# Attention and a mixture of experts on one core: the subtractions that form the low parts of the second-layer weights, moved from GpSimd to VectorE for experts 2 to 7

## The chip, the cores and the metric

The kernel runs on one core of one Trainium2 chip. The metric is the device time of one execution in microseconds; for the kernel before, three runs were timed. A separate execution was taken with the hardware profiler, and every time of the trace is counted from the start of its span.

## The reference, cut to what matters

Eight batches of 2496 tokens with 256 channels go through an attention whose weights are squared positive scores. Each of the 19968 resulting rows that passes a skip test is given to one of eight experts, a two-layer network of 256, 1024 and 256 channels, and the expert's output is added with a gate.

```
scores = (1 / S) * z @ z.T ; attn = maximum(scores, 0) ** 2
x = u * (attn @ v)
xc = x[x @ w_skip > 0]
e_idx = argmax(xc @ w_gate) ; gate_w = softmax(xc @ w_gate)[e_idx]
for e in range(8):
    h = maximum(xc[e_idx == e] @ w1[e], 0)
    y[e_idx == e] = gate_w * (h @ w2[e])
out[x @ w_skip > 0] = xc + y
```

All is float32. The kernel gets near that accuracy by splitting each matmul operand into a high part (a cast to the fp32r format) and a low part (the rest) and by adding three products: high by high, high by low, low by high.

## The kernel before, in words

**Two stages.** The attention goes through 40 chunks of up to 512 queries (to about 1250 us of the trace). Routing writes the tokens' numbers and gates into one list per expert in DRAM. Then the experts are worked through one after the other.

**An expert.** Of each expert's list, the first 768 tokens are worked in three *fixed units* of 256 tokens (NFIX = 3, `unit(e, 4, ...)`, i = 0, 1, 2), and the rest in the arm of a `tc.Switch` (line 1034) on the number of further blocks of 64 tokens, in units of up to 512 tokens. All five engines branch at the Switch; each loads the arm's number (line 1027) and gives a prefetch hint (line 1028) in the third fixed unit.

**A unit.** `fetch` (lines 639 and 641) copies token numbers to `go` on VectorE, and GpSimd gathers the rows xgf or xgu by indirect DMA. `turn_pe` (lines 659 to 662) transposes them on TensorE into pst; ScalarE writes the high part xt and VectorE the low part. Then `h_part` p computes psh with 24 matmuls for a fixed unit (line 693; four psh buffers), ScalarE writes hh (line 698) and VectorE hl (line 699). `y_part` adds up the second layer in y (line 712). VectorE forms o (line 741) and GpSimd scatters it into the output by indirect DMA (line 744). For a fixed unit the order is h0, h1, h2, h3, y0, y1, y2 and y3 in one; these are the slots 0 to 6, and a table `fills` hangs other work behind a slot.

**Weights.** While expert e is worked, the weights of e + 1 are brought in eight pieces by `load_w` (called once per expert; the pieces are hung behind slots 1, 3 and 5 of the fixed units). Pieces 0 to 3 are w1, pieces 4 to 7 are w2. For a piece, SP loads a raw tile of 128 x 512 (line 97, four raw buffers, three pieces ahead); ScalarE casts the high part (line 152 for w1h, 158 for w2t); the low part is a subtraction (line 153 for w1l, one of 128 x 512; line 159 for w2t, two of 128 x 256). The engine of the subtraction is `load_w`'s second argument:

```
wq = load_w(e + 1, nc.gpsimd if e else nc.vector) if more else []
```

So the weights of experts 0 and 1 have their subtractions on VectorE, those of experts 2 to 7 on GpSimd. For e from 1 to 6 the pieces 0 to 2 stand in the first fixed unit, 3 to 5 in the second (piece 4 behind slot 3, piece 5 behind slot 5), 6 and 7 in the third (behind slots 1 and 3).

**The order of the work.** The schedule is manual: each engine runs its instructions in the order in which the code writes them, so an instruction that waits holds up all that its engine has behind it.

## Time and profile before

| what | value |
|---|---|
| three timed runs | 1748.35, 1749.15, 1760.32 us; median 1749.15 |
| the profiled execution | 1752.5 us, span 1750.7 us, mean clock 0.997 |
| attention stage (0 to 1218 us) | TensorE busy 1208.1 us, VectorE 982.6, ScalarE 941.3, GpSimd 257.1 |
| one expert (1354 to 1412 us) | TensorE busy 58.0 of 58 us, VectorE 21.4, ScalarE 19.1, GpSimd 35.2 |
| another (1474 to 1543 us) | TensorE busy 67.8 of 69 us, VectorE 27.7, ScalarE 21.9, GpSimd 37.8 |

In the tables of the profile, PE is TensorE, PEld its weight loads, DVE VectorE, ACT ScalarE, POOL GpSimd and SP the engine that issues most DMAs. A row of a timeline gives the start, the duration, the engine, the line, the operation, the tiles written and read, how many are merged in the row, and in brackets the idle time of that engine just before and what ended it. "issue" means that nothing that the profile shows ended it.

### The profile page before, as it was taken

The numbers are of one execution on the slowest core, as the hardware profiler recorded it, in microseconds if no ns is written. First come the engines' busy times: TensorE is split into PE (matmuls) and PEld (weight loads), VectorE is DVE, ScalarE is ACT, GpSimd is POOL, SyncE is SP. The second block draws the span as 40 slices with busy tenths as digits, with TensorE's granted clock in tenths as the row PEclk, the third lists the DMA queues.
The fourth block names the chain that finished last, engine by engine and source line by source line (L and its number), as shares of the span: only waits on it lengthen the run. The fifth ranks groups of instructions, "written<-read, shape, count | busy, mean of one in ns | idle before, by whom it ended". The sixth has DMA issues, their size and how long they took to land.

```text
span 1750.7 us, 39411 instructions
## 1 busy us (share of the span) xinstructions
PE 1725.2 (99%) x15474; PEld 1526.5 (87%) x15474; DVE 1204.1 (69%) x1976; ACT 1111.2 (63%) x1409; POOL 516.6 (30%) x516
## 2 busy tenths in 40 slices
PE   9999999999999999999999999999999999999998
PEld 7888889988888898888988887888889989999997
DVE  7877877887787788788878877877743334343432
ACT  8877876887687688778768875877333323333321
POOL 1103202211220321132132112112346546645731
PEclk9999999999999999999999999999999999999999
DMA  5586699589869957986896899589543324323210
GB/s 188 151 219 176 174 255 282 145 227 256 210 155 251 278 156 220 266 222 154 247 257 167 217 273 230 144 223 241 163 117 86 90 79 106 91 60 95 85 41 27
DMA packets 424972, 307.32 MB, mean 176 GB/s; under 512 B 187888, under 2 KB 362865, under 8 KB 424016
## 3 DMA queue, kind: packets, MB, share of 16 engines
q1 hardware_dynamic: 410592, 280.44, 59.0%
q0 software_dynamic: 13632, 22.99, 4.7%
q8 instruction: 137, 2.24, 0.5%
q14 instruction: 179, 1.47, 0.3%
q10 hardware_dynamic: 432, 0.18, 0.0%
HBM read 184.21 MB, written 140.08 MB: 185 GB/s over the span
## 4 chain that ended last, share of the span: by engine, by line
PE 86%; DMA 7%; ACT 2%; issue 2%; DVE 2%; SPq 0%; another core or an unknown queue 0%; POOL 0%; POOLq 0%; DVEq 0%; ACTq 0%
PE acc L421 53%; PE y L712 11%; PE psh L693 11%; PE ps L302 8%; DMA r<-kept 3%; DMA out<-o,idt 2%; DMA out<-xr 1%; PE psm L493 1%; PE pst L659 1%; DVE al L392 1%; ACT ah L388 1%; PE ps L285 0%; ACT r L379 0%; DMA raw<-in_v 0%; ACT r L378 0%
## 5 line engine op out<-in xcount | busy, mean ns | idle before, releaser
L421 PE MATMUL acc<-ah,vh 64*128 64x512 f32 (+1 forms) x3120 | 640.4, 384 | 3.7 <-DVE ah L388 2.5
L421 PE MATMUL acc<-ah,vl 64*128 64x512 f32 (+1 forms) x3120 | 625.6, 382 | 0.0
L392 DVE TENSOR_TENSOR al<-r,ah 128x1024 fp32r<-128x1024 f32 (+1 forms) x400 | 479.7, 1205 | 152.6 <-ACT ah L388 128.3
L421 PE MATMUL acc<-al,vh 64*128 64x512 f32 (+1 forms) x3120 | 497.8, 384 | 3.4 <-DVE al L392 3.1
L592 POOL DMA_INDIRECT lst<-pair,dest x160 | 199.5, 1247 | 781.0 <-DVE dest L590 752.2
L388 ACT CAST ah<-r 128x1024 fp32r<-128x1024 f32 (+1 forms) x356 | 362.9, 1029 | 105.6 <-DMA r<-kept 71.9
L421 PEld LDWEIGHTS acc<-ah,vh 64*128 64x128 f32 x3120 | 325.7, 184 | 55.2 <-DVE ah L388 3.7
L421 PEld LDWEIGHTS acc<-ah,vl 64*128 64x128 f32 x3120 | 326.1, 184 | 44.1 <-DVE vl L122 0.3
L421 PEld LDWEIGHTS acc<-al,vh 64*128 64x128 f32 x3120 | 308.1, 184 | 58.8 <-DVE al L392 13.8
L378 ACT ACTIVATE r<-ps 128x1024 f32<-128x1024 f32 (+1 forms) x224 | 228.0, 1018 | 127.8 <-PE ps L302 112.1
L698 ACT ACTIVATE hh<-psh 128x512 fp32r<-128x512 f32 (+2 forms) x172 | 96.1, 572 | 290.9 <-PE psh L693 243.9
L379 ACT ACTIVATE r<-r 128x1024 f32<-128x1024 f32 (+1 forms) x224 | 235.9, 1053 | 7.1
L712 PE MATMUL y<-w2t,hh 128*128 128x256 f32 (+1 forms) x1328 | 237.6, 282 | 0.6 <-issue 0.4
L699 DVE SCALAR_TENSOR_TENSOR hl<-psh,hh 128x512 fp32r<-128x512 f32 (+2 forms) x172 | 110.0, 655 | 155.7 <-ACT hh L698 112.7
L712 PEld LDWEIGHTS y<-w2t,hh 128*128 128x128 f32 (+1 forms) x1328 | 202.6, 187 | 3.0 <-issue 0.9
L319 DVE STREAM_TRANSPOSE rt<-r 128x512 f32<-128x512 f32 x304 | 197.4, 687 | 11.1 <-DMA kept<-rt 11.1
L693 PE MATMUL psh<-xt,w1h 128*128 128x256 f32 (+3 forms) x896 | 185.1, 304 | 7.1 <-DVE hl L699 4.5
L712 PE MATMUL y<-w2t,hl 128*128 128x256 f32 (+1 forms) x664 | 185.4, 279 | 0.7 <-DVE hl L699 0.7
L693 PEld LDWEIGHTS psh<-xt,w1h 128*128 128x128 f32 x896 | 141.9, 189 | 13.2 <-DVE hl L699 5.9
L693 PE MATMUL psh<-xt,w1l 128*128 128x256 f32 (+3 forms) x448 | 135.3, 302 | 0.0
L744 POOL DMA_INDIRECT out<-o,idt x77 | 76.5, 994 | 167.3 <-DVE o L741 134.4
L712 PEld LDWEIGHTS y<-w2t,hl 128*128 128x128 f32 (+1 forms) x664 | 123.8, 186 | 0.9 <-DVE hl L699 0.9
(197 smaller groups left out, 1740.2 us busy)
## 6 DMA issues: line engine op xcount, KB each, us to landing
kept<-rt SPq DMA_DIRECT2D x304, 256.0 KB
r<-kept SPq DMA_DIRECT2D x90, 512.0 KB
r<-kept SPq DMA_DIRECT2D x62, 352.0 KB
raw<-in_v SPq DMA_DIRECT2D x80, 256.0 KB
ut<-in_uT SPq DMA_DIRECT2D x32, 512.0 KB
xr<-xrow SPq DMA_DIRECT2D x128, 128.0 KB
out<-xr SPq DMA_DIRECT2D x32, 512.0 KB
raw<-in_w SPq DMA_DIRECT2D x64, 256.0 KB
```

The lines of the kernel that those rows point to most:

```text
L302: nc.tensor.matmul(to, k[h, o : o + P], queries(ci, q, h, n), start=(m == 0), stop=(m == 2))
L319: nc.vector.transpose(t[:, :, 32 * k : 32 * k + 32].rearrange("p (k a) i -> p a k i", k=4), r[:, x, :].rearrange("p (a k i) -> p a k i", a ...
L378: nc.scalar.activation(r[:, :, :n], ps[:, :, :n], AF.Relu, scale=isc)
L379: nc.scalar.activation(r[:, :, :n], r[:, :, :n], AF.Square)
L388: (nc.scalar.copy if on_act(ci, p) else nc.vector.tensor_copy)(h_, r_)
L392: nc.vector.tensor_sub(l_, r_, f32(h_))
L421: nc.tensor.matmul(acc[t][:, :n], w[h, x, dd], a[h, x, :n], start=(first and t not in halves[:m]), stop=(last and t not in halves[m + 1 :]),)
L592: put = nc.gpsimd.indirect_dma_start(out=lst, out_offset=bass.IndirectOffsetOnAxis(ap=dest[:, t : t + 1], axis=0), in_=pair[:, t, :], in_o ...
L693: nc.tensor.matmul(ps[:, j * W : (j + 1) * W], wt[:, a, o : o + P], x[:, d, :W], start=(m == 0), stop=(m == 5),)
L698: nc.scalar.activation(hh[:, : G * W], ps[:, : G * W], AF.Relu)
L699: nc.vector.scalar_tensor_tensor(hl[:, : G * W], ps[:, : G * W], 0.0, f32(hh[:, : G * W]), op0=ALU.max, op1=ALU.subtract)
L712: nc.tensor.matmul(ys[t], h[:, tt], w2t[f][:, k, :], start=(f == 0 and m == 0 and t % share == 0), stop=(f == NF - 1 and m == 2), skip_gro ...
```

## The change

The second-layer subtraction is no longer given to the engine that `load_w` is called with; it always goes to VectorE. The w1 pieces keep their engine: GpSimd for experts 2 to 7.

```
                     nc.scalar.copy(t[:, 0, :], r[:, a, :])
-                    eng.tensor_sub(t[:, 1, :], r[:, a, :], f32(t[:, 0, :]))
+                    nc.vector.tensor_sub(t[:, 1, :], r[:, a, :], f32(t[:, 0, :]))
```

For six experts with four w2 pieces of two subtractions each, that is 48 instructions. TensorE, ScalarE and SP keep their order.

On VectorE, from the second half of expert 1's second fixed unit into its third (idt_203 and idt_202 are the token lists of experts 2 and 1; xt_17906 is a tile of turned rows):

```order
 L699 SCALAR_TENSOR_TENSOR hl<-psh,hh 128x512 x2
 L662 TENSOR_TENSOR xt_17906<-pst,xt_17906 128x2x256
+L159 TENSOR_TENSOR w2t<-raw,w2t 128x256 x2
 L639 COPY go<-idt_203 128x2
+L159 TENSOR_TENSOR w2t<-raw,w2t 128x256 x2
 L741 SCALAR_TENSOR_TENSOR o<-y,idt_202,xgf 128x256 x2
 L1027 TENSOR_LOAD arm
 L699 SCALAR_TENSOR_TENSOR hl<-psh,hh 128x512 x2
 L639 COPY go<-idt_202 128x2
+L159 TENSOR_TENSOR w2t<-raw,w2t 128x256 x2
 L1028 SWITCH_STRIDE
 L1028 ISA
```

Pieces 4 and 5 stand ahead of an index copy and of o; piece 6 stands between the second hl and the third, which follows the hint.

Later in the same third unit on VectorE (from its third hl to the second turned tile for the Switch):

```order
 L699 SCALAR_TENSOR_TENSOR hl<-psh,hh 128x512 x2
 L662 TENSOR_TENSOR xt_17907<-pst,xt_17907 128x2x256
+L159 TENSOR_TENSOR w2t<-raw,w2t 128x256 x2
 L639 COPY go<-idt_203 128x2
 L662 TENSOR_TENSOR xt_17907<-pst,xt_17907 128x2x256
```

Piece 7 stands between the two turned tiles.

On GpSimd, the same stretch (xgf and xgu are gathered rows, out the scatter):

```order
 L153 TENSOR_TENSOR w1l<-raw,w1h 128x512
-L159 TENSOR_TENSOR w2t<-raw,w2t 128x256 x2
 L641 DMA xgf<-xr,go 128x256 x2
-L159 TENSOR_TENSOR w2t<-raw,w2t 128x256 x2
 L744 DMA out<-o,idt_202 19968x256 x2
 L1027 TENSOR_LOAD arm
 L641 DMA xgu<-xr,go 128x256 x2
-L159 TENSOR_TENSOR w2t<-raw,w2t 128x256 x2
 L1028 SWITCH_STRIDE
 L1028 ISA
 L1028 BRANCH_PREFETCH_HINT
-L159 TENSOR_TENSOR w2t<-raw,w2t 128x256 x2
```

All four pairs are gone; of the tensor work, w1l stays between the gathers and scatters.

## The prediction

> **What bounds the kernel now.** I read the page's busy times first, then the busy times by stage from the stage where the changed instructions run, then who waited for whom there, then the ends of the idle spells one by one.

> ```profile
> PE 1725.2 (99%) x15474; PEld 1526.5 (87%) x15474; DVE 1204.1 (69%) x1976; ACT 1111.2 (63%) x1409; POOL 516.6 (30%) x516
> ```

> TensorE works nearly always; GpSimd's 30% is a mean over two unlike stages. The stage that matters runs from about 1300 us (first Switch) to 1693 us (end of the last expert's fixed units): all 48 affected subtractions lie in it, as their row below shows (1346.6 to 1648.9 us). The columns are length, then busy us (and count) of PE, PEld, DVE, ACT and POOL, then clock and DMA.

> ```profile
> 1300.00:1693.00 393.00, 386.66 (x3130) 379.56 (x3129) 151.15 (x286) 125.16 (x252) 211.32 (x218) 1.00 0.30 83
> 1693.00:1751.00 58.00, 51.07 (x394) 48.66 (x392) 18.59 (x32) 11.47 (x20) 13.73 (x14) 0.98 0.11 34
> 1412.00:1474.00 62.00, 60.17 (x457) 57.56 (x456) 22.56 (x41) 19.05 (x38) 35.65 (x38) 0.97 0.34 91
> ```

> In the stage TensorE is idle for 393.00 - 386.66 = 6.3 us only. VectorE is busy 151.15/393 = 38%, GpSimd 54%. No engine but TensorE is near a bound. The tail after 1693 us belongs to the last expert, which loads no weights for a successor, so the change has no instruction there. What ended TensorE's 6.3 us (the waits of that stage, PE rows; total, times, longest):

> ```profile
> PE psh L693 <- DVE hl L699: 4.5, 3, 1.8
> PE psh L693 <- issue: 1.8, 1, 1.8
> ```

> 4.5 + 1.8 = 6.3: four waits hold all of it. None is for GpSimd, for a gather or for a weight tile. One of them lies behind expert 0's Switch:

> ```profile
> 1302.33 0.67 PE L693 MATMUL psh<-xt,w1h 128*128 128x448 f32 x2 [1.50 <-DVE hl L699]
> ```

> Expert 0's code forms expert 1's weights on VectorE already, so this 1.50 us is no business of the change; 6.3 - 1.5 = 4.8 us in three waits are left. These follow late starts of ScalarE behind a Switch; the rows of two of them, and of a Switch without such a wait:

> ```profile
> 1417.70 2.06 ACT L698 ACTIVATE hh<-psh 128x512 fp32r<-128x512 f32 x4 [3.73 <-issue]
> ...
> 1478.38 1.85 ACT L698 ACTIVATE hh<-psh 128x448 fp32r<-128x448 f32 x4 [4.11 <-issue]
> ...
> 1357.46 1.59 ACT L698 ACTIVATE hh<-psh 128x512 fp32r<-128x512 f32 x3 [2.65 <-issue]
> ```

> The idle time in brackets is ScalarE's, and "issue" says that nothing in the profile released it. Where it is 3.73 and 4.11 us, all four psh buffers are full and TensorE waits; where it is 2.65 us (a Switch of the same kind, one expert earlier), TensorE does not. So what is left to gain here is ScalarE's branch time, not GpSimd's work.

> **The change part by part.**

> ```profile
> L159 POOL TENSOR_TENSOR w2t<-raw,w2t 128x256 fp32r<-128x256 f32 x48 | 34.2, 742 | 0.3
> L153 POOL TENSOR_TENSOR w1l<-raw,w1h 128x512 fp32r<-128x512 f32 x24 | 30.9, 1302 | 0.5
> ...
> L159 DVE TENSOR_TENSOR w2t<-raw,w2t x16: 415/419/423, 1218.4 to 1294.9; 128x256 fp32r<-128x256 f32 x16
> ```

> Removed from GpSimd: 48 subtractions of 742 ns, 34.2 us busy; its share of the stage falls from 54% to (211.3 - 34.2)/393 = 45%. Added to VectorE: 48 of the same shape; the 16 that it already runs took 419 ns, so 48 x 0.419 = 20.1 us, and its share rises from 38% to 44%. The DMAs, ScalarE's casts and TensorE's order stay as they are. GpSimd keeps the 24 subtractions w1l of 1.30 us.

> What this costs on the path is decided by what stands behind the subtractions in VectorE's queue. Per expert there are four pairs. Two (pieces 4 and 5) stand where VectorE next has a tiny index copy and then the end of a unit. The tight ones are pieces 6 and 7, in the third fixed unit: piece 6 stands ahead of the third hl, piece 7 ahead of the second xt. Here is that place in one expert (VectorE, ScalarE's casts, then the chain with TensorE's groups):

> ```profile
> 1403.80 0.16 DVE L639 COPY go<-idt 128x2 int32<-128x2 int32 x1
> 1404.60 0.69 DVE L699 SCALAR_TENSOR_TENSOR hl<-psh,hh 128x512 fp32r<-128x512 f32 x1 [0.65 <-ACT hh L698]
> 1406.30 0.69 DVE L699 SCALAR_TENSOR_TENSOR hl<-psh,hh 128x512 fp32r<-128x512 f32 x1 [1.00 <-issue]
> 1407.03 0.69 DVE L662 TENSOR_TENSOR xt<-pst,xt 128x512 fp32r<-128x512 f32 x1
> 1407.64 0.16 DVE L639 COPY go<-idt 128x2 int32<-128x2 int32 x1
> 1409.62 0.69 DVE L662 TENSOR_TENSOR xt<-pst,xt 128x512 fp32r<-128x512 f32 x1 [1.82 <-ACT xt L661]
> ```

> ```profile
> 1403.05 0.70 ACT L158 CAST w2t<-raw 128x256 fp32r<-128x256 f32 x2
> ```

> ```profile
> 1405.78 2.74 PE y L712 x24
> 1408.52 0.44 PE pst L659 x4
> 1408.96 2.74 PE y L712 x24
> 1411.70 0.44 PE pst L659 x4
> 1412.14 0.93 PE psh L693 x4
> ```

> Piece 6: its casts end at 1403.75, the index copy at 1403.96. A pair of subtractions takes at most 2 x 0.42 = 0.84 us, so it ends at 1404.80 and the third hl starts at 1404.80 instead of 1404.60: 0.2 us late. That hl is read by the y group that starts at 1408.96; it would end at 1405.5, over 3 us ahead. The fourth hl starts at 1406.30 as before. Piece 7: it follows the xt at 1407.03, ends at about 1408.6, and the second xt starts at 1409.62 as before, ending 1.8 us before the Switch's first psh at 1412.14. Cost on the path: 0.0 us. The work that hides it is TensorE's own y groups; were they gone, the cost would be 6 experts x 2 pairs x 0.84 = 10 us.

> What the relief of GpSimd is worth: it works far behind its place in the code.

> ```profile
> 1400.69 1.31 POOL L153 TENSOR_TENSOR w1l<-raw,w1h 128x512 fp32r<-128x512 f32 x1
> 1401.94 1.44 POOL L159 TENSOR_TENSOR w2t<-raw,w2t 128x256 fp32r<-128x256 f32 x2
> ```

> The pair at 1401.94 is piece 4, which belongs to the second fixed unit and runs in the third. Its gathers and scatters will now go out up to 8 x 0.71 = 5.7 us sooner per expert. But no wait of TensorE in the stage ends with a gather, so this is worth 0.0 us too. The raw buffers of w2 come free sooner as well; the last of w1's subtractions stays on GpSimd, and it is that one which frees the buffer of piece 7.

> [...] The rows: a VectorE subtraction with two SBUF inputs takes 684 ns in the median and up to 1101; one of the long ones ran under a GpSimd cast. The index copy, 0.16 us above, took 1.28 us under a w1l. Two subtractions of the very kind that is moved, under a gather, took 0.75 together, no more than alone.

> ```profile
> L122 DVE TENSOR_TENSOR vl<-raw,vh x80: 647/684/1101, 5.1 to 1092.2; 128x512 fp32r<-128x512 f32 x80
> ```

> ```profile
> 288.05 1.10 DVE L122 TENSOR_TENSOR vl<-raw,vh 128x512 fp32r<-128x512 f32 x1
> ```

> ```profile
> 287.52 1.09 POOL L263 CAST zqh<-zh 128x512 fp32r<-128x512 f32 x1 [8.29 <-PE ps L285]
> ```

> ```profile
> 1453.66 1.28 DVE L639 COPY go<-idt 128x2 int32<-128x2 int32 x1
> ```

> ```profile
> 1453.59 1.30 POOL L153 TENSOR_TENSOR w1l<-raw,w1h 128x512 fp32r<-128x512 f32 x1
> ```

> ```profile
> 1294.57 0.75 DVE L159 TENSOR_TENSOR w2t<-raw,w2t 128x256 fp32r<-128x256 f32 x2
> ```

> ```profile
> 1294.46 1.00 POOL L641 DMA_INDIRECT xgf<-xr,go  x1 [0.30 <-issue]
> ```

> So a moved pair can be held by a w1l that runs: bounds 0 and 1.30 us. I take near 0 for most: GpSimd has 24 w1l against 24 pairs, and busy with them only 30.9 of 393 us. Even the full 1.30 at piece 6 makes the third hl 1.5 us late, inside its 3 us. [...]

> Sum against the profiled execution: 1752.5 us (span 1750.7 and 1.8 around it) + 0.0 + 0.0 = 1752.5. It lies 3.35 us above the median of the three runs, 1749.15, so for a median I forecast **1749 us**, own range 1745 to 1753 for shifts of the three waits by a microsecond each.

> **The rivals.**
> *Faster by the Switch.* GpSimd's gathers leave the DMA queues sooner, and ScalarE's code for the arm arrives sooner. Then the three waits vanish: -4.8 us, and the dip of the clock behind the longest one (0.97 over 62 us, 1.9 us): 1749.1 - 6.7 = 1742.4 us. For it: 3.73 and 4.11 us against 2.65 show that ScalarE's time behind a Switch varies. Against: ScalarE's row names no releaser, and GpSimd works on through the quiet Switch too. [...]

> *Slower by the Switch.* VectorE's longer and GpSimd's shorter code shift what is fetched when, and the three quiet Switches of experts 1, 4 and 6 stall like the worst: 3 x (1.8 + 1.9) = 11.1 us, 1760 us. It decides from a gap of ScalarE somewhere between 2.65 and 3.73 us on. Against: ScalarE's instructions do not change.

> [...]

> *The change does not do what it says*: the pairs wait on VectorE for ScalarE's casts or the raw DMA, and the index copies and gathers behind them come late. Then GpSimd gains nothing, but TensorE still never waited for a gather: 1749 us again.

> **How the numbers follow.** Hidden altogether 0.75 (1749 us), hidden though the pairs wait 0.04 (the same time), faster by the Switch 0.09 (1742.4), slower by the Switch 0.07 (1760), by the port 0.05 (1762). The range 1742 to 1757 holds the first three and reaches towards the slower ones; it leaves out most of the last two. A measurement of this kernel tells about 1% (17.5 us) from no change. None of the cases gets there; 0.02 for faster and 0.03 for slower are left for what no row shows, 0.95 for the same.

> **What would show it.** In the changed kernel L159 on GpSimd is gone and on VectorE counts 64 with a median near 0.42 us; a few pairs stretch towards 1.7 us under a w1l. TensorE's idle time from 1300 to 1693 us stays near 6 us and sits behind Switches. GpSimd's w1l and gathers start sooner. I am wrong if TensorE waits for hl or xt inside a fixed unit, if a w2t pair is named as what TensorE waits for, or if the waits behind the Switches grow or go.

## The result and the profile after

| kernel | median | runs | lowest to highest |
|---|---|---|---|
| before | 1750.88 us | 20 | 1746.73 to 1760.32 |
| changed | 1766.35 us | 20 | 1757.6 to 1772.59 |

The ratio is 1.0086, with a 95% interval of 1.0076 to 1.0096: 15.5 us slower. That is inside the 1% that the forecast called "the same" and outside its range of times (1742 to 1757). The profiled execution took 1764.64 us with a span of 1762.8 us, against 1752.5 and 1750.7 before, so 12.1 us of span are there to be explained.

The page of the changed kernel, and the instructions of the moved line (count; shortest, median and longest in ns; first and last start):

```profile
PE 1730.4 (98%) x15474; PEld 1534.1 (87%) x15474; DVE 1219.3 (69%) x2024; ACT 1111.6 (63%) x1409; POOL 485.5 (28%) x468
```

```profile
L159 DVE TENSOR_TENSOR w2t<-raw,w2t x64: 411/418/1732, 1214.7 to 1657.9; 128x256 fp32r<-128x256 f32 x64
```

The move itself is as forecast: 48 instructions have left GpSimd (516 to 468; 516.6 to 485.5 us busy) and joined VectorE (1976 to 2024), with a median of 418 ns. TensorE has the same 15474 matmuls. Now the stage of the experts to the end of the last fixed units, and the tail, in the columns of the prediction's table:

```profile
1300.00:1705.00 405.00, 391.55 (x3123) 382.69 (x3124) 165.18 (x332) 124.77 (x252) 177.70 (x168) 0.99 0.28 77
1705.00:1763.00 58.00, 51.23 (x395) 48.83 (x393) 18.80 (x32) 11.63 (x21) 13.14 (x14) 0.96 0.11 34
```

TensorE is idle for 405.00 - 391.55 = 13.5 us of the stage, where it was 6.3. What ended these waits (PE rows; total, times, longest):

```profile
PE y L712 <- issue: 6.7, 10, 1.0
PE psh L693 <- DVE hl L699: 3.4, 3, 2.4
PE psh L693 <- issue: 3.3, 3, 1.9
PE pst L659 <- issue: 0.8, 1, 0.8
```

The two psh rows, the waits behind Switches, add up to 6.7 us, as good as the 6.3 of before. New are 6.7 + 0.8 us in eleven short waits inside the y groups and the turn next to them, and nothing in the profile released them. They lie in third fixed units. Nine of the eleven (6.4 of the 7.5 us) stand before matmuls whose records name no semaphore to wait for, and neither do those of the weight loads that go with them: there TensorE waited for no tile at all, it stood still. One such place, in expert 4, on ScalarE, TensorE and GpSimd:

```profile
1527.59 0.60 ACT L698 ACTIVATE hh<-psh 128x512 fp32r<-128x512 f32 x1 [1.65 <-PE psh L693]
1528.08 0.71 ACT L158 CAST w2t<-raw 128x256 fp32r<-128x256 f32 x2
1533.46 1.09 ACT L698 ACTIVATE hh<-psh 128x512 fp32r<-128x512 f32 x2 [4.68 <-remote]
```

```profile
1527.85 0.28 PE L693 MATMUL psh<-xt,w1l 128*128 128x256 f32 x1
...
1531.98 0.28 PE L712 MATMUL y<-w2t,hl 128*128 128x256 f32 x1 [0.75 <-issue]
1532.10 0.28 PE L712 MATMUL y<-w2t,hh 128*128 128x256 f32 x1
1533.43 0.47 PE L712 MATMUL y<-w2t,hh 128*128 128x256 f32 x1 [1.05 <-issue]
```

```profile
1524.74 1.01 POOL L641 DMA_INDIRECT xgf<-xr,go  x1 [0.16 <-DVE o L741]
1526.06 1.01 POOL L641 DMA_INDIRECT xgf<-xr,go  x1 [0.30 <-issue]
1527.37 1.03 POOL L744 DMA_INDIRECT out<-o,idt  x1 [0.31 <-issue]
1528.71 1.00 POOL L744 DMA_INDIRECT out<-o,idt  x1 [0.31 <-issue]
1530.02 1.05 POOL L641 DMA_INDIRECT xgu<-xr,go  x1 [0.30 <-issue]
1531.38 1.01 POOL L641 DMA_INDIRECT xgu<-xr,go  x1 [0.30 <-issue]
```

The third hh waits for the psh whose last matmul started at 1527.85 (a psh of a fixed unit takes 12 matmuls in the trace, not the 24 of the text ahead of the prediction), and starts at 1533.46: 5.6 us later, with ScalarE idle for 4.68 of them. VectorE's hl follows. TensorE's two waits here, of 0.75 and 1.05 us, do not: they stand before matmuls that name no semaphore. And TensorE's signals themselves are late. Of the four that follow the one at 1527.57 on record, the first came at 1533.44 and the last at 1533.65, though the matmuls that send them had ended from 1528.13 to 1529.98. So the late hh and TensorE's idle time stand side by side, as two signs of something that held TensorE. The granted clock was 0.83 over the 10 us from 1530. GpSimd meanwhile issues six gathers and scatters in an unbroken run, one every 1.3 to 1.4 us; in the kernel before a pair of subtractions stood in this run:

```profile
1522.48 1.01 POOL L641 DMA_INDIRECT xgf<-xr,go  x1 [0.31 <-issue]
1523.52 1.43 POOL L159 TENSOR_TENSOR w2t<-raw,w2t 128x256 fp32r<-128x256 f32 x2
1525.11 1.04 POOL L744 DMA_INDIRECT out<-o,idt  x1 [0.17 <-issue]
```

The sum, from 1270 to 1730 us, in the changed kernel and in the one before:

```profile
1270.00:1730.00 460.00, 442.92 (x3499) 431.25 (x3498) 190.98 (x388) 142.09 (x287) 201.81 (x191) 0.99 0.29 81
```

```profile
1270.00:1730.00 460.00, 452.37 (x3615) 442.12 (x3614) 180.27 (x345) 144.81 (x291) 236.02 (x241) 0.99 0.30 82
```

TensorE's idle time went from 7.6 to 17.1 us. Behind the longer spells the granted clock is lower for some microseconds; six of the 46 stretches of 10 us are under 1.00 in the changed kernel, the first and the last of them being

```profile
1280.00:1290.00 10.00, 7.24 (x50) 6.66 (x49) 2.96 (x7) 3.33 (x9) 5.28 (x5) 0.89 0.55 143
...
1530.00:1540.00 10.00, 8.21 (x57) 8.00 (x57) 3.33 (x7) 2.76 (x6) 4.06 (x4) 0.83 0.56 161
```

(1 - clock) x 10 us adds up to 6.8 us over these six, against 3.5 in the kernel before. 9.5 us more idle and 3.3 us more at the lower clock are 12.8 us, against the 12.1 of the spans. So the loss is idle spells of TensorE and the clock behind them, most of it in third units. But 2.3 of the 9.5 us lie between 1270 and 1300 us, in expert 0, where both kernels run the same instructions; they are not the change's.

### The profile page after: what moved, and what is told of

It is laid out like the page before. It is cut to its first block, busy times and chain, and to the rows that moved or that the text cites. A ratio compares the mean times of both kernels' runs of the same rounds, so it can differ in the third digit from the quotient of the medians.

```text
span 1762.8 us, 39410 instructions
## 1 busy us (share of the span) xinstructions
PE 1730.4 (98%) x15474; PEld 1534.1 (87%) x15474; DVE 1219.3 (69%) x2024; ACT 1111.6 (63%) x1409; POOL 485.5 (28%) x468
## 4 chain that ended last, share of the span: by engine, by line
PE 86%; DMA 5%; issue 4%; ACT 2%; DVE 2%; SPq 1%; POOL 1%; another core or an unknown queue 0%; POOLq 0%; ACTq 0%; DVEq 0%
PE acc L421 53%; PE y L712 11%; PE psh L693 10%; PE ps L302 8%; DMA out<-o,idt 2%; DMA r<-kept 2%; PE psm L493 1%; PE pst L659 1%; DMA raw<-in_v 1%; DVE al L392 1%; ACT ah L388 1%; PE ps L285 0%; DMA out<-xr 0%; ACT r L379 0%; ACT r L378 0%
## 5 line engine op out<-in xcount | busy, mean ns | idle before, releaser
L698 ACT ACTIVATE hh<-psh 128x512 fp32r<-128x512 f32 (+2 forms) x172 | 96.2, 572 | 311.0 <-PE psh L693 238.7
L712 PE MATMUL y<-w2t,hh 128*128 128x256 f32 (+1 forms) x1328 | 239.4, 282 | 5.9 <-issue 5.9
L699 DVE SCALAR_TENSOR_TENSOR hl<-psh,hh 128x512 fp32r<-128x512 f32 (+2 forms) x172 | 110.2, 655 | 175.6 <-ACT hh L698 130.1
L712 PEld LDWEIGHTS y<-w2t,hh 128*128 128x128 f32 (+1 forms) x1328 | 203.5, 187 | 9.5 <-issue 7.2
L319 DVE STREAM_TRANSPOSE rt<-r 128x512 f32<-128x512 f32 x304 | 197.3, 687 | 10.8 <-DMA kept<-rt 10.8
L693 PE MATMUL psh<-xt,w1h 128*128 128x256 f32 (+3 forms) x896 | 186.5, 305 | 6.7 <-DVE hl L699 3.4
L712 PE MATMUL y<-w2t,hl 128*128 128x256 f32 (+1 forms) x664 | 185.8, 280 | 3.8 <-issue 3.0
L693 PEld LDWEIGHTS psh<-xt,w1h 128*128 128x128 f32 x896 | 143.0, 190 | 13.8 <-issue 5.2
L693 PE MATMUL psh<-xt,w1l 128*128 128x256 f32 (+3 forms) x448 | 136.0, 304 | 0.0
L712 PEld LDWEIGHTS y<-w2t,hl 128*128 128x128 f32 (+1 forms) x664 | 123.9, 187 | 3.9 <-issue 2.9
```

Source lines behind the costliest of these rows:

```text
L319: nc.vector.transpose(t[:, :, 32 * k : 32 * k + 32].rearrange("p (k a) i -> p a k i", k=4), r[:, x, :].rearrange("p (a k i) -> p a k i", a ...
L693: nc.tensor.matmul(ps[:, j * W : (j + 1) * W], wt[:, a, o : o + P], x[:, d, :W], start=(m == 0), stop=(m == 5),)
L698: nc.scalar.activation(hh[:, : G * W], ps[:, : G * W], AF.Relu)
L699: nc.vector.scalar_tensor_tensor(hl[:, : G * W], ps[:, : G * W], 0.0, f32(hh[:, : G * W]), op0=ALU.max, op1=ALU.subtract)
L712: nc.tensor.matmul(ys[t], h[:, tt], w2t[f][:, k, :], start=(f == 0 and m == 0 and t % share == 0), stop=(f == NF - 1 and m == 2), skip_gro ...
```

## The experiments

Every experiment was timed beside the kernel before on the same chip; the kernels of one set shared a chip. Ratios are to the kernel before of the set, with 95% intervals.

### One half of the move at a time

Theory A: GpSimd, relieved, reaches its gathers and scatters sooner, and these meet the prefetch hints of the third fixed unit. Theory B: VectorE's 20 us more hold up hl and xt. Theory C: the subtractions on VectorE contend with GpSimd's tensor work. `pool_pad` keeps GpSimd's load beside the changed kernel; nobody reads what it writes:

```
                     nc.vector.tensor_sub(t[:, 1, :], r[:, a, :], f32(t[:, 0, :]))
+                    if eng is nc.gpsimd:
+                        nc.gpsimd.tensor_sub(scr[0][:, 0, :D], r[:, a, :], f32(t[:, 0, :]))
```

> The changed kernel, with GpSimd still running 48 subtractions of the same inputs at the old places, into a scratch tile that nobody reads; VectorE forms the real low parts. So VectorE has the whole new load and GpSimd none of the relief. Theory A (the time is lost because GpSimd, relieved, issues its gathers and scatters sooner and in one burst, into the stretch of the third fixed unit in which the engines give their prefetch hints): about 1751 us, as before. Theory B (the added 20 us on VectorE hold up hl and xt): about 1766 us. [...]

Measured: 1740.62 us against 1742.85, ratio 0.9981 (0.9965 to 0.9998). VectorE's load costs nothing where GpSimd is as busy as before. B and C fall, as far as this set goes; A's 1751 us, as the kernel before, is what came.

`act_low` relieves GpSimd and gives VectorE nothing; it leaves the low parts of the second-layer weights of experts 2 to 7 out:

```
+                    if eng is nc.gpsimd:
+                        nc.scalar.mul(t[:, 1, :], r[:, a, :], 0.0)
+                    else:
                         nc.vector.tensor_sub(...)
```

> The changed kernel, but for experts 2 to 7 the low part of w2 is neither subtracted on GpSimd nor on VectorE: ScalarE writes it as the raw tile times zero, so the low parts of these second layers are left out of the result. GpSimd is relieved, VectorE gets nothing. Theory A: slow like the changed kernel, about 1766 us (ScalarE's 48 x 0.41 = 20 us stand behind its own casts). Theory B and theory C: about 1751 us, unless ScalarE's own load delays hh, which would show as waits for hh inside the fixed units.

Measured: 1744.09 us, 1.001 (0.999 to 1.0031). The relief alone cost nothing here either, though the run of six gathers and scatters was as unbroken as in the changed kernel. So theory A, which had 1766 us here, fell too, and I took that to mean that only both together cost something. That set had no run of the changed kernel itself, which the next one made good.

### Without the hints

Both kernels without the prefetch hint of line 1028. The page of the kernel before has two DMA queues of the kind "instruction":

```profile
q8 instruction: 137, 2.24, 0.5%
q14 instruction: 179, 1.47, 0.3%
```

In expert 2 the engines run their hints from 1400.7 to 1406.1 us. In the 10 us from 1400.7 on six packets of these queues move, in the 10 us ahead of it none. What a branch waits for, no row shows. The edit:

```
-                add(fills, (1, lambda: tc.switch_hint({g: n for g in ENGINES}, narms, label="rest%d" % e)))
...
-        for arm in tc.Switch(n, narms, hint="rest%d" % e):
+        for arm in tc.Switch(n, narms):
```

> [...] Theory A with the hints as the thing that is collided with: the gaps inside the third fixed unit vanish (5 to 7 us of PE idle), but every Switch costs more: so nearer to the kernel before without hints than the 15 us between the two kernels with hints. If the difference between this kernel and the kernel before without hints is still about 15 us, the hints have no part in it.

> The kernel before without the prefetch hints: the control for the changed kernel without them. All theories: slower than 1751 us by what a branch without a hint costs in eight experts (an estimate of 0 to 3 us each from ScalarE's 2.65 to 4.11 us behind a Switch, so 1751 to 1775 us). Theory A: within 5 us of the changed kernel without hints. Theories B and C: 15 us faster than it.

Measured: changed without hints 1777.66 us, 1.0209 (1.016 to 1.0257); before without hints 1766.21 us, 1.0131 (1.009 to 1.0171). TensorE's largest wait from 1270 to 1730 us, first of the changed, then of the kernel before:

```profile
PE psh L693 <- issue: 29.4, 7, 6.5
```

```profile
PE psh L693 <- issue: 22.5, 8, 4.2
```

The hint is worth about 23 us to the kernel before. Without it the change costs 11.5 us, 6.9 of them (29.4 - 22.5) in these waits at the Switches. That is another place than the y groups, where neither of these two profiles has a wait; whether the loss there needs the hint, this set doesn't tell.

### The changed kernel on a second chip, code, operands and place of the hint

> The changed kernel once more, with nothing edited, on the chip of the three that follow. The loss needs both GpSimd without the pairs' work and the subtractions on VectorE: VectorE's load alone gave 0.9981 and GpSimd's relief alone 1.001. Three theories are left for why. F, code: VectorE's program is 56 instructions longer and GpSimd's 56 shorter, so what is fetched as code, and when, changes. G, place of the hints: the code that the hint calls in the third fixed unit arrives while GpSimd issues six gathers and scatters without a break, and TensorE is silent for 4 to 7 us there. H, VectorE's reading: a subtraction that reads two operands of SBUF on VectorE while GpSimd prepares indirect DMAs holds GpSimd or TensorE up. All three expect 1.0086 here, within 1.005 to 1.012, and in the profile PE idle spells of about 0.5 to 1 us in pairs in the y groups of third units. If it comes out within 1.003 of before, the loss hangs on the chip.

Measured: 1748.26 us against 1743.42, 1.0027 (1.0011 to 1.0044), on chip 10; the chip of the first result isn't on record. (The 56 instructions of this expectation and of one below are 48 in the trace.) The ratio is within the 1.003 named for the case that the loss hangs on the chip, and it took the ground from under the first set: `pool_pad` and `act_low` had been compared with a loss that perhaps wasn't there. Its profile has none of the paired spells in y groups: of 10.8 us of idle time between 1270 and 1730 us, 9.2 stand behind Switches, where TensorE waits for hl. The same place as above, on ScalarE, TensorE and GpSimd:

```profile
1517.45 0.60 ACT L698 ACTIVATE hh<-psh 128x512 fp32r<-128x512 f32 x1 [0.81 <-PE psh L693]
1517.94 0.70 ACT L158 CAST w2t<-raw 128x256 fp32r<-128x256 f32 x2
1518.86 0.60 ACT L698 ACTIVATE hh<-psh 128x512 fp32r<-128x512 f32 x1 [0.22 <-PE psh L693]
1520.27 0.60 ACT L698 ACTIVATE hh<-psh 128x512 fp32r<-128x512 f32 x1 [0.81 <-PE psh L693]
```

```profile
1518.54 0.28 PE L693 MATMUL psh<-xt,w1l 128*128 128x256 f32 x1
```

```profile
1515.04 1.01 POOL L641 DMA_INDIRECT xgf<-xr,go  x1 [0.16 <-issue]
...
1521.71 1.02 POOL L641 DMA_INDIRECT xgu<-xr,go  x1 [0.30 <-issue]
```

The program is the same, GpSimd's run (six from 1515.04 to 1521.71) is the same, and the third hh starts 0.32 us behind its matmul in place of 5.6. So the late hh isn't made by the program alone. The small loss of this set, as far as one profile tells, lies behind Switches, at another place than the first one.

`dve_one` (experts 2 to 7 get raw times zero, one operand, in the place of the subtraction; their second layer's low parts are left out), `pool_stub` (the changed kernel with GpSimd subtracting 2 columns at the old places) and `hint3` (the hint behind slot 3):

```
+                    if eng is nc.gpsimd:
+                        nc.vector.tensor_scalar_mul(t[:, 1, :], r[:, a, :], 0.0)
```

```
+                    if eng is nc.gpsimd:
+                        nc.gpsimd.tensor_sub(scr[0][:, 0, :2], r[:, a, :2], f32(t[:, 0, :2]))
```

```
-                add(fills, (1, lambda: tc.switch_hint(
+                add(fills, (3, lambda: tc.switch_hint(
```

> The changed kernel, but for experts 2 to 7 VectorE writes the low part of a second-layer weight as its raw value times zero: an instruction with one operand from SBUF in the place of the subtraction's two, at the same place in the program, with the same waits for the cast but for the one on the copy. The low parts of these experts' second-layer weights are left out. H expects the loss gone: 0.998 to 1.003. F, with the same number of instructions on every engine, expects it kept: 1.006 to 1.012. G expects it kept where the durations are alike (the row of the new operation will tell; if it takes half of the 0.42 us, VectorE's hint comes 0.2 to 0.4 us sooner, and G allows 1.000 to 1.009).

> The changed kernel with GpSimd subtracting 2 columns of the same operands in place of 256, at the old places of the subtractions, into scratch that nobody reads: GpSimd keeps its 56 instructions and their waits for ScalarE's casts, but is relieved of nearly all their time. F expects the loss gone, since GpSimd's program is as long as before: 0.998 to 1.002, as with the full-size dummy subtractions (0.9981). H expects it kept, since GpSimd spends its time on indirect DMAs as in the changed kernel: 1.005 to 1.010. G expects what the distances between the gathers become: if the six still go in one unbroken run of 1.3 us each, 1.005 to 1.010, and if the waits for the casts break the run as before, 0.998 to 1.003.

> The changed kernel with the hint two y groups later: at slot 3 of the third fixed unit in place of slot 1, so that the code is fetched some 6 us later, behind most of GpSimd's run of gathers and scatters and still some 10 us ahead of the Switch. G expects the loss gone or mostly so: 0.997 to 1.004, and no silence of TensorE's semaphore over 4 us around the hint's fetch. F and H expect 1.005 to 1.012, with the silent spells where they were. A new loss at the Switches (a fetch that is late there) would show as PE gaps of over 1 us at the Switch's lines and is told apart by that.

Measured: 1.002 (1.0 to 1.0039), 1.0007 (0.9993 to 1.0021) and 1.0029 (1.0012 to 1.0046). `pool_stub` lies under the control, though the intervals overlap; the other two can't be told from a control of 1.0027. The ranges on record for F, G and H were made for a loss of 0.86%. That F's holds `pool_stub`, H's `dve_one`, and G's, with its conditions, all three numbers, says nothing here: the set was too quiet to rule on the spells of the first profile.

### Which pairs, and code or waits

> The changed kernel once more, unedited, as the control of the three that follow. It gave 1.0086 when it was first timed and 1.0027 on another chip. In the two profiles the loss has two forms: idle time of TensorE (between 1270 and 1730 us 17.1 us in the first, 10.8 in the second, 7.6 in the kernel before) and, behind the longer spells, stretches at a granted clock of 0.78 to 0.99 (worth 6.8, 5.1 and 3.5 us). If the size hangs on the chip, 1.002 to 1.009 here; if the first figure was the odd one, 1.001 to 1.004.

Measured: 1746.28 us against 1742.01, 1.0017 (1.0004 to 1.0031).

`late67` and `early45` (k < 6 in the place of k >= 6) move one half of the pairs each; `pool_free` is `pool_stub` with a write of 2 columns that waits for nobody:

```
-                    eng.tensor_sub(t[:, 1, :], r[:, a, :], f32(t[:, 0, :]))
+                    (nc.vector if k >= 6 else eng).tensor_sub(t[:, 1, :], r[:, a, :], f32(t[:, 0, :]))
```

```
-                        nc.gpsimd.tensor_sub(scr[0][:, 0, :2], r[:, a, :2], f32(t[:, 0, :2]))
+                        nc.gpsimd.memset(scr[0][:, 0, :2], 0.0)
```

> Of the changed kernel only the pairs of pieces 6 and 7 stay on VectorE, the two that lie around the hint in the third fixed unit of experts 2 to 7; those of pieces 4 and 5, in the second unit, go back to GpSimd. Place theory: the loss comes from the third unit, where GpSimd's gathers and scatters run without a break around the hint and GpSimd comes to the Switch early, so all of the control's loss is here: within 0.0015 of its ratio. Sum theory: what counts is GpSimd's or VectorE's total, so about half of the control's loss: 1.001 to 1.002 if the control is at 1.0027, 1.003 to 1.005 if it is at 1.0086.

> The other half: pieces 4 and 5 on VectorE, pieces 6 and 7 back on GpSimd, so that the third fixed unit of experts 2 to 7 is as in the kernel before. Place theory: no loss, 0.998 to 1.001. Sum theory: about half of the control's loss.

> The changed kernel with GpSimd writing 2 columns of zeros to scratch at each of the old places: as many instructions as with the 2-column subtractions (1.0007), but with no operand from ScalarE's cast, so without the waits. Code theory (GpSimd's shorter program is what costs): as the 2-column subtractions, 0.999 to 1.002. Waits theory (a GpSimd that no longer waits for ScalarE's casts runs ahead to its gathers, and that costs): as the control, 1.002 to 1.009.

Measured: `late67` 1.0036 (1.0022 to 1.005), `early45` 0.9989 (0.9975 to 1.0003), `pool_free` 1.0022 (1.0008 to 1.0035). `early45` is where the place theory had it; `late67` lies above the range of both theories (the place theory allowed 0.0015 from the control's 1.0017). In this set the small loss is with the pairs of pieces 6 and 7, and GpSimd's instructions without their waits don't take it away; the intervals of `late67`, `pool_free` and the control overlap. That spoke for a GpSimd that runs ahead, and for the way that remained, the Switch.

### GpSimd held back at the Switch

In the profiles up to here, ScalarE's time behind the Switch of expert 2 was long where GpSimd's branch came right behind its own, and short where GpSimd came late: TensorE idled there for 0.8 to 2.2 us in seven runs with GpSimd's branch 4.5 to 4.9 us behind TensorE's, and for 0.0 to 0.5 us in four with 6.8 us or more. So GpSimd was delayed there by copies within scratch, ten (`after_l10`, and `before_l10` on the kernel before) or six (`after_l6`):

```
                 add(fills, (7, lambda: turn_pe(pair(e + 1, 0), turned(e + 1, 0))))
+                if e:
+                    add(fills, (7, lambda: [nc.gpsimd.tensor_copy(scr[0][:, 1, :], scr[0][:, 0, :]) for _ in range(10)]))
```

> The changed kernel, unedited, as the control of the three that follow. Between 1.0017 and 1.0027 as on the last two chips, or 1.0086 as on the first, if this chip is like it.

> The changed kernel with ten copies of 128x512 within scratch on GpSimd (0.8 to 0.9 us each by the rows of the cast of that size) at the end of the third fixed unit of experts 1 to 6, ahead of its last scatter. Switch theory: what costs on these chips is that a GpSimd without the pairs comes to the Switch 4.5 us behind TensorE's branch, right behind ScalarE's at 2.1 and VectorE's at 2.9, so that the code of three engines is fetched at once and ScalarE resumes 4 to 6 us behind its branch in place of 2.5 to 3; hh is late then, TensorE idles up to 3 us in the unit behind the Switch, and its clock falls behind the longer spells. At expert 2 the profiles so far show an idle spell of 0.0 to 0.5 us in four runs in which GpSimd's branch came 6.8 us or more behind TensorE's, and of 0.8 to 2.2 in seven in which it came at 4.5 to 4.9. It expects GpSimd's branch at 9 us or later here, ScalarE's resumption within 2.5 to 3.9 us at experts 1 to 4, and 0.997 to 1.000, under the control by 0.002 or more. Third-unit theory: what costs is that the gathers and scatters ahead of the Switch run without a break, which this edit leaves as it is: the control's ratio, and if the late scatter holds up o, more.

> The same with six copies: GpSimd's branch at about 7 to 8 us behind TensorE's. Switch theory: between the control and the kernel with ten copies, nearer to the latter (0.998 to 1.001). Third-unit theory: the control's ratio.

> The kernel before with the same ten copies. There GpSimd's branch comes at 4.6 to 5.6 us behind TensorE's too, and TensorE idled 1.5, 0, 1.8, 1.2, 0, 1.8 and 0 us behind the Switches of experts 0 to 6. Switch theory: 0.997 to 1.000 here as well, since it isn't the change that brings the loss but the place of GpSimd's branch. Third-unit theory: 1.000 to 1.003, for the late scatter alone.

Measured: control 1.0008 (0.999 to 1.0025), `after_l10` 1.001 (0.9996 to 1.0025), `after_l6` 1.0004 (0.9989 to 1.0019), `before_l10` 0.9997 (0.9983 to 1.001). The control has hardly a loss to take away, so that `after_l6` and `before_l10` lie in the Switch theory's ranges means little, but the mechanism can be read all the same. ScalarE and GpSimd of `after_l10` at expert 2:

```profile
1409.93 2.07 ACT L698 ACTIVATE hh<-psh 128x512 fp32r<-128x512 f32 x4 [5.12 <-PE psh L693]
```

```profile
1404.87 6.71 POOL L1029 COPY scr<-scr 128x512 f32<-128x512 f32 x10
1412.27 1.05 POOL L744 DMA_INDIRECT out<-o,idt  x1 [0.69 <-DVE hl L699]
```

and ScalarE of the control:

```profile
1408.60 2.07 ACT L698 ACTIVATE hh<-psh 128x512 fp32r<-128x512 f32 x4 [5.40 <-PE psh L693]
```

GpSimd is held back until 1412, and ScalarE is as late as in the control (5.12 and 5.40 us idle, four hh at once). The Switch theory falls; what it rested on was an agreement of eleven profiles at one place.

### The large loss again

> The changed kernel, unedited, on one more chip. Chip theory: the size of the loss belongs to the chip. In the profile of the first timing (1.0086) ScalarE starts hh 1.7 to 3.8 us behind the last matmul that it waits for at seven places of the expert stage, and in the profiles of three other chips (1.0027, 1.0017, 1.0008) at one place, none and none. It expects 1.000 to 1.003 here with none or one such place, or, on a chip like the first, 1.006 to 1.011 with five or more of them. If the ratio comes out above 1.005 without such places, or under 1.003 with five of them, the theory falls.

> The pairs of pieces 4 and 5 alone on VectorE, once more, beside the changed kernel and with more rounds; it gave 0.9989 [0.9975, 1.0003]. Place theory (the loss comes with the pairs of pieces 6 and 7 in the third fixed unit): 0.998 to 1.000 on any chip, also on one like the first, where the late starts of hh lie in third units. If it is slower than 1.001, the place theory falls; if it is under 0.999 with its whole interval under 1, it is a version that beats both kernels.

Measured: the changed kernel 1767.18 us against 1750.95, 1.0086 (1.0069 to 1.0104), the first result over again; `early45` 1762.77 us, 1.0076 (1.0055 to 1.0096), against 0.9989 in the third set. Call a start late where ScalarE takes up a tile of TensorE over 1.5 us behind both the last matmul that signals and its own work before. Between 1270 and 1730 us the control has seven, `early45_b` six; in the profile of the first result there were seven, in the kernel before none, in the other three controls one, none and none. Waits before matmuls that name no semaphore, in y groups and turns from 1300 us on, stand at 12 places in the control, at 11 in `early45_b`, at nine in the first result's profile, and at none in the other 17 profiles. So the size goes with both signs, and both belong to the set. That leaving the third unit alone would avoid them, the place theory, falls. The same place in the two runs of `early45`, ScalarE and GpSimd; in the last set

```profile
1524.50 0.60 ACT L698 ACTIVATE hh<-psh 128x512 fp32r<-128x512 f32 x1 [1.65 <-PE psh L693]
1524.99 0.70 ACT L158 CAST w2t<-raw 128x256 fp32r<-128x256 f32 x2
1530.37 1.09 ACT L698 ACTIVATE hh<-psh 128x512 fp32r<-128x512 f32 x2 [4.68 <-remote]
```

```profile
1525.63 1.00 POOL L744 DMA_INDIRECT out<-o,idt  x1 [0.31 <-issue]
1526.93 1.04 POOL L641 DMA_INDIRECT xgu<-xr,go  x1 [0.30 <-issue]
1528.28 1.01 POOL L641 DMA_INDIRECT xgu<-xr,go  x1 [0.30 <-issue]
1529.31 1.42 POOL L159 TENSOR_TENSOR w2t<-raw,w2t 128x256 fp32r<-128x256 f32 x2
```

and in the third set:

```profile
1507.95 0.60 ACT L698 ACTIVATE hh<-psh 128x512 fp32r<-128x512 f32 x1 [0.81 <-PE psh L693]
1508.45 0.70 ACT L158 CAST w2t<-raw 128x256 fp32r<-128x256 f32 x2
1509.36 0.60 ACT L698 ACTIVATE hh<-psh 128x512 fp32r<-128x512 f32 x1 [0.22 <-PE psh L693]
```

In `early45` VectorE has none of the moved pairs in the third unit, and still hh is late there. What differs from the kernel before at this place is GpSimd alone: without the pairs of pieces 4 and 5 its six gathers and scatters follow one another without a break.

The sets that had the changed kernel:

| set | before | changed | ratio | late starts | TensorE signals on record, of 1365 | of these late |
|---|---|---|---|---|---|---|
| first result | 1750.88 | 1766.35 | 1.0086 | 7 | 1274 | 37 |
| second chip | 1743.42 | 1748.26 | 1.0027 | 1 | 1366 | 0 |
| third | 1742.01 | 1746.28 | 1.0017 | 0 | 1367 | 0 |
| fourth | 1739.08 | 1741.33 | 1.0008 | 0 | 1365 | 0 |
| last | 1750.95 | 1767.18 | 1.0086 | 7 | 1294 | 43 |

The sixth column counts the trace's semaphore records for the signals that TensorE's instructions carry (the end of the program adds up to two). The profile of the kernel before that the prediction rests on has 1278, and `early45_b` 1284: the four profiles of the first and the last set lack 5 to 7% of them, the other 16 none. The last column counts the records, up to 1735 us, that came over 0.7 us behind the end of the last matmul that signals. `early45_b` has 41 of them, and the kernel before 19, up to 1.8 us late; the other 16 profiles have none, and no record there is later than 0.32 us.

So the kernel before was not free of it in the first set. In expert 0, where GpSimd has no subtraction of the second layer in either kernel, ScalarE, TensorE and GpSimd of the kernel before show

```profile
1284.38 0.60 ACT L698 ACTIVATE hh<-psh 128x512 fp32r<-128x512 f32 x1 [8.43 <-PE psh L693]
```

```profile
1280.79 0.28 PE L693 MATMUL psh<-xt,w1l 128*128 128x256 f32 x1
```

```profile
1279.92 1.02 POOL L641 DMA_INDIRECT xgu<-xr,go  x1 [0.30 <-issue]
...
1283.86 1.03 POOL L744 DMA_INDIRECT out<-o,idte  x1 [0.30 <-issue]
```

This hh starts 3.59 us behind the last matmul of its psh, during a run of gathers and scatters that no tensor work breaks. It isn't among the late starts above because a later matmul had signalled in between. From the experts' first hh to the first one behind expert 0's Switch the four profiles take 44.7 to 48.5 us, the other 16 take 38.9 to 42.5: that accounts for a part of the difference between 1751 us and 1742 us for the kernel before.

**What is settled, and what stays open.** Settled: the loss of 0.86% comes back, in one kind of set and not in the other, with the same program; it consists of idle spells of TensorE and lower clock, and most of the spells in y groups stand where TensorE waits for nothing that the program asks for. In that kind of set TensorE's signals come late in both kernels, and about twice as often in the changed one (37 and 43 records against 19). In the three other sets the change costs 2 to 5 us. Not settled: what holds TensorE and its signals. A lead is this: in six of these places (experts 4 and 5 of the first result, of the control and of `early45` in the last set) hh starts 2.08, 2.00, 1.90, 2.12, 2.09 and 2.13 us behind the start of the last gather of GpSimd's run (for instance 1531.38 to 1533.46 above). Of all 20 late starts in the three profiles, 12 come 1.9 to 2.2 us behind the start of a run's last gather or scatter, seven 0.5 to 1.0 us and one 2.4 us behind the start of one. So a late hh often comes free when the run ends, and in the kernel before, whose run is broken by a pair in third units, hh is late in expert 0, where the run is unbroken. But the same unbroken run makes nothing late in the other kind, and neither a kernel with GpSimd relieved and its run broken (`pool_stub`) nor one with VectorE's load and GpSimd's run as before (`pool_pad`) was timed in a set of the first kind; that would decide it. The results number the chip of the last set like that of the first experiments, where the kernel before took 1742.85 us with all records there, so the kind isn't fixed to that number.

No version beats both kernels. `pool_pad` with 0.9981 comes nearest, in one quiet set; `early45` with 0.9989 is at 1.0076 in the other kind.

## Why the prediction was wrong

**Removed and added: right.** 48 instructions moved, VectorE's at a median of 418 ns where 419 was taken. VectorE's busy time rose by 15.2 us where 20.1 was expected; what became shorter no run isolates.

**Piece 6 and 7, "cost on the path: 0.0 us": right, as far as the runs go, for VectorE's own time.** `pool_pad` has the whole load of VectorE and isn't slower (0.9981), in a set of the quiet kind. And in the last set hh is late in third units in which `early45` gives VectorE nothing.

**"What the relief of GpSimd is worth: 0.0 us": the step that failed.** The argument was that no wait of TensorE ends with a gather, so gathers that go out sooner change nothing. It priced only waits for a result, and took TensorE to stand still nowhere else. What the runs showed in its place: 6.4 of the 7.5 us of new waits in y groups and turns stand before matmuls that wait for no semaphore, and TensorE's signals reach ScalarE late (the hh at 1533.46 starts 5.6 us behind the start of its last matmul, 0.3 us on the second chip). The argument also left out what the freed 5.7 us per expert do to GpSimd's pattern: six gathers and scatters without a break, where a pair stood in them. `early45`, which relieves GpSimd of half the pairs and gives VectorE nothing in the third unit, has the same stalls there and costs 11.8 us (1.0076). So this is the term that was mis-sized: 0.0 us foretold, 15.5 and 16.2 us in two sets, 2.3, 4.3 and 4.8 in three. That the run itself holds TensorE is argued, not shown; the cause stays open.

**The sum's reference.** The forecast of 1749 us took one level for the kernel before. It is 1739 to 1743 us in four sets and 1751 in two, so a set alone shifts a time by 12 us, most of the 15 us of the range that was given (1742 to 1757). The chances left 0.75 for 1749 us, and counted no stall that the trace of the kernel before did not name.

**The rivals.** The 1762 us that the chances list *by the port* (0.05) came nearest in time to 1766.35, by luck. That VectorE and GpSimd meet at a port, no run shows. What the runs show is one subtraction that stretched to 1732 ns under a w1l, as foretold, in expert 1's second unit; TensorE waited for no hl inside a fixed unit, and in `pool_pad` VectorE's load alone is free (0.9981). *Slower by the Switch* (1760 us) looked for stalls that no row releases, but at the Switches, where the waits stayed at 6.7 against 6.3 us; in the second chip's profile (9.2 us) and without hints (6.9 us more) its place is right. *Faster by the Switch* didn't happen. That *the pairs wait for ScalarE's casts* is true for 1.9 us in all, and no wait of TensorE names a pair.

**What would show it.** "TensorE's idle time stays near 6 us" was the sign that failed, with 13.5. The list of signs had waits for hl, for xt and for w2t; it had none without a releaser inside a fixed unit.

## What to carry to other kernels

Taking work off an engine that otherwise only issues DMAs also takes away the pauses between its DMAs (here six in one run, one every 1.3 to 1.4 us): ask what the new pattern may do, not only whether somebody waits for the DMA's data. Where an engine stands idle, look first whether the instruction behind the gap waits for anything at all; if not, no producer is to blame. A loss under 1% should be seen in two sets on different chips before it is explained, and every set of experiments needs the changed kernel itself as a control, since here the loss was there or not by the set. A mechanism read off ten profiles (GpSimd's branch and ScalarE's lateness) can be chance; move the suspected event alone before believing it. And count a trace's semaphore records against the signals of the program: here four profiles with missing records are the four with late signals.

## What the runs showed of the hardware

The prefetch hint on five engines is worth 1.3% to this kernel (1766.21 us without it against 1742.85, 1.0131).

TensorE's granted clock fell behind an idle spell of 2.5 us in the control on the second chip (to 0.84 over 10 us, worth 1.6 us) and stayed at 1.00 behind spells of 2.1 and 2.7 us in `hint3`, on the same chip; so spells of this length can cost themselves alone, or more than half as much again.
